# Attention in halves of 64 tokens: eight small score tiles at once, half as many weighted scores, two state steps per block

## The chip, the cores and the metric

The kernel runs on one core of one Trainium2 chip. The metric is the device time of one execution in microseconds (us). A run of the program is longer than its span in the profile, because some time lies before the first and after the last instruction that the profile shows.

## The reference, cut to what matters

The inputs are x (4 batches, 8 heads, 768 tokens, 32 values), a decay a per token, and B and C (16 values per token). The attention is linear with decay; the reference works in chunks of 32 tokens:

```python
cum = np.cumsum(la, axis=-1)                      # la = log(a) of the chunk
L = np.exp(cum[:, :, :, None] - cum[:, :, None, :]) * causal
M = np.einsum('bhin,bhjn->bhij', Cc, Bc) * L      # scores, weighted
y = einsum(M, xc) + einsum(Cc, state) * exp(cum)  # inside the chunk + from the state
state = decay_full * state + sum_j(Bc * xc * decay_from_j)
```

The result is independent of the size of the chunk. Behind it stands a feed-forward layer over the 256 values of a token (8 heads of 32): normalise with the gain g, multiply by w1 (256 x 1024), relu, multiply by w2 (1024 x 256), add the input. The weights come as 64-bit pairs of words and are rebuilt in the kernel.

## The kernel before, in words

The 768 tokens are worked in six blocks t = 0 to 5 of 128 tokens; a block of all four batches is 512 columns. Inside a block the decays are kept per sub-block of 32 tokens (SUB). Nothing is planned at run time: a list of 645 steps, ISSUE, is written out in full, and each engine and the DMA queue of SyncE (SP) execute their own steps strictly in that order. A step that waits holds up everything behind it on its engine. A step's name stands for a function (L496 to L505 hold the table).

Attention of a block, in the names of the steps:

- `C`, `cm`, `B` (L318 to L334) scale C and B by decays inside a sub-block; `cm` parts the heads into even and odd ones. `c2` (L336) is C for the state's part, `be` (L342) is B decayed to the end of the block.
- `W` (L347) copies the decays between sub-blocks into the weights WW, with three copies on ScalarE for each half u of the batches.
- `G t u` (score, L352) is TensorE's: for each of two batches and each pair of heads q, B (32 rows, 128 columns of weights) against C of two heads (256 columns). Four pairs of heads lie in four groups of 32 rows of the array. A block needs `G t 0` and `G t 1`, each with four tiles of PSUM.
- `R t u q` (weighted, L364) is one VectorE multiplication of a PSUM tile (128 x 512) by WW: eight per block.
- `V t n` (value, L369) makes y for batches n and 2+n: for t > 0 first the state's part (L382: 32 rows, 64 columns of weights, 128 columns streamed), then the part inside the block (L387: 128 rows, 32 columns of weights, 128 columns streamed).
- `Z t` (carry, L390) sums B times x over the 128 tokens (128 rows, 32 columns, 64 columns streamed); `K` (L399) and `S` (L403) step the state once per block on VectorE, `sb` (L410) masks the state by head.
- `y`, `yh`, `yl`, `T`, `tc` copy y out of PSUM, split it in two parts, and turn it to tokens; `st`, `ag`, `rs`, `rc` are the statistics of the normalisation.

Every multiplication of fp32 operands on TensorE appears in the trace as two matmul records, each with its own load of weights; those of fp32r operands as one.

The feed-forward layer of a block is `h t m` (hidden, L459; eight per block, six matmuls of 512 columns each), `hh` on ScalarE and `hl` on VectorE, then `o t b` (outputs, L475; four per block, 24 matmuls of 256 columns each), `oe` on VectorE and the store `od`. The weights are prepared ahead of the first block: `k0` to `k3`, `kr`, `f` rebuild a quarter of w1 or w2, `wc`, `wh`, `wl` centre and split it. `fill` (L489) is a matmul of zeros whose result nobody reads. PSUM has five buffers for the attention (`att`) and three for everything else (`ffn`).

## Time and profile before

| what | value |
|---|---|
| three runs: median (lowest, highest) | 208.12 us (207.79, 210.56) |
| the profiled execution's own time | 208.15 us |
| its span, first to last instruction | 206.1 us |
| granted TensorE clock, mean of the span | 0.975 of full |
| TensorE matmul (PE) busy | 194.9 us, 95%, 1,874 records |
| VectorE (DVE) busy | 134.8 us, 65%, 280 instructions |
| ScalarE (ACT) busy | 88.1 us, 43%, 166 instructions |
| GpSimd (POOL) busy | 30.2 us, 15%, 29 instructions |

The ends of matmul records are modelled and records overlap, so a sum of their busy times is more than the time they hold TensorE. The chain of work that ended last gives the time of a group of records from its first start to the start of the next group; those figures add up to the span.

### The profile page before, as it was taken

To read this page: it belongs to the slowest core of one execution; us is meant where nothing else is said; L and a number is where in the kernel's file an instruction comes from. 1 tells how busy PE (TensorE), PEld (TensorE's weight loads), DVE (VectorE), ACT (ScalarE), POOL (GpSimd) and SP (SyncE) were. 2 spreads that over 40 slices of the span, in tenths; PEclk is the share of its full clock that TensorE was granted. 3 is DMA by queue.
4 is the path that set the end of the run, shared out by engine and by line. 5 is a ranking of instruction groups with operands and counts; after the bars stand their busy time and mean duration, and the time that the engine had idled before them with its cause. 6 is when DMAs were issued, how large, how long until landed. Compare 5 with 4: busy or idle time off the path is not lost.

```text
span 206.1 us, 4484 instructions
## 1 busy us (share of the span) xinstructions
PE 194.9 (95%) x1874; PEld 163.5 (79%) x1874; DVE 134.8 (65%) x280; ACT 88.1 (43%) x166; POOL 30.2 (15%) x29
## 2 busy tenths in 40 slices
PE   8359999989999999999999999999999999999993
PEld 8246555759887788889877999779898799988993
DVE  5689999999959998747449813662634651547310
ACT  3799897951553875223425212352033310145100
POOL 0216254432261213000000000004000000000000
PEclk9955999999999999999999999999999999999999
DMA  5899974143646020010003011000000001000011
GB/s 160 257 380 390 386 268 151 54 124 101 226 147 241 32 70 38 0 56 27 25 3 102 3 51 51 3 0 29 25 25 29 0 25 49 5 29 2 3 49 51
DMA packets 12180, 18.90 MB, mean 92 GB/s; under 512 B 2528, under 2 KB 6144, under 8 KB 12160
## 3 DMA queue, kind: packets, MB, share of 16 engines
q1 hardware_dynamic: 12160, 18.62, 26.4%
q8 instruction: 14, 0.23, 0.5%
q14 instruction: 6, 0.05, 0.1%
HBM read 15.31 MB, written 3.31 MB: 90 GB/s over the span
## 4 chain that ended last, share of the span: by engine, by line
PE 80%; DVE 7%; DMA 4%; ACT 4%; SPq 2%; issue 2%; ACTq 0%
PE po L480 34%; PE ph L465 28%; PE G L360 6%; PE yps L387 5%; DMA b<-in_bn_dram 4%; PE yps L382 3%; PE yt L434 2%; PE wc L214 2%; DVE R L366 1%; ACT top L178 1%; DVE cs L320 1%; ACT WW L350 1%; PE Z L396 1%; ACT hh L469 1%; ACT L453 1%
## 5 line engine op out<-in xcount | busy, mean ns | idle before, releaser
L480 PE MATMUL po<-w,hh 128*128 128x256 f32 x384 | 68.9, 282 | 0.0
L480 PEld LDWEIGHTS po<-w,hh 128*128 128x128 f32 x384 | 58.7, 188 | 2.9 <-issue 1.9
L465 PE MATMUL ph<-yh,w 128*128 128x512 f32 x192 | 53.6, 401 | 0.9 <-DVE hl L473 0.8
L480 PE MATMUL po<-w,hl 128*128 128x256 f32 x192 | 53.6, 279 | 0.0
L469 ACT ACTIVATE hh<-ph 128x512 fp32r<-128x512 f32 x48 | 28.6, 597 | 55.0 <-PE ph L465 49.9
L473 DVE SCALAR_TENSOR_TENSOR hl<-ph,hh 128x512 fp32r<-128x512 f32 x48 | 32.8, 687 | 21.2 <-ACT hh L469 20.9
L465 PEld LDWEIGHTS ph<-yh,w 128*128 128x128 f32 x192 | 34.3, 188 | 10.0 <-DVE hl L473 1.5
L480 PEld LDWEIGHTS po<-w,hl 128*128 128x128 f32 x192 | 36.1, 188 | 0.0
L484 DVE SCALAR_TENSOR_TENSOR o<-po,rstd,ytok 128x256 f32<-128x256 f32 x24 | 11.5, 481 | 30.5 <-PE po L480 30.5
L366 DVE TENSOR_TENSOR R<-G,WW 128x512 f32<-128x512 f32 x48 | 30.5, 679 | 0.7 <-PE G L360 0.6
L465 PE MATMUL ph<-yl,w 128*128 128x512 f32 x96 | 30.0, 392 | 0.3 <-DVE yl L427 0.3
L350 ACT COPY WW<-wt 32x512 f32<-32x512 f32 (+2 forms) x36 | 19.8, 613 | 17.5 <-DVE R L366 13.6
L465 PEld LDWEIGHTS ph<-yl,w 128*128 128x128 f32 x96 | 18.0, 188 | 4.6 <-DVE yl L427 0.7
L360 PE MATMUL G<-cm,bs 32*128 32x256 f32 x192 | 16.0, 443 | 1.0 <-DVE bs L334 1.0
L360 PEld LDWEIGHTS G<-cm,bs 32*128 32x128 f32 x192 | 10.3, 207 | 4.2 <-issue 1.6
L202 POOL TENSOR_TENSOR top<-top,raw 128x512 int32<-128x512 int32 x8 | 11.2, 1402 | 15.8 <-DVE top L192 7.8
L427 POOL TENSOR_TENSOR yl<-y,yh 128x512 fp32r<-128x512 f32 x3 | 3.8, 1283 | 61.9 <-DVE yh L424 61.9
L387 PE MATMUL yps<-R,xt 128*32 128x128 f32 x384 | 12.8, 275 | 0.1
L387 PEld LDWEIGHTS yps<-R,xt 128*32 128x32 f32 x384 | 9.8, 109 | 1.9 <-issue 1.9
L418 ACT COPY y<-yps 128x256 f32<-128x256 f32 x13 | 4.4, 369 | 14.0 <-PE yps L387 13.8
L446 DVE BATCH_NORM_STATS2 st<-ytok 128x6 f32<-128x256 f32 x24 | 9.2, 415 | 1.7 <-ACT ytok L439 1.7
L439 ACT COPY ytok<-yt 128x512 f32<-128x512 f32 x12 | 7.0, 581 | 4.2 <-PE yt L434 4.2
(87 smaller groups left out, 173.6 us busy)
## 6 DMA issues: line engine op xcount, KB each, us to landing
raw<-in_w_dram SPq DMA_DIRECT2D x8, 512.0 KB, 7.0
xt<-in_x_dram SPq DMA_DIRECT2D x6, 512.0 KB, 5.3
out_dram<-o SPq DMA_DIRECT2D x24, 128.0 KB, 1.7
ud<-scr SPq DMA_DIRECT2D x10, 256.0 KB
c<-in_cn_dram SPq DMA_DIRECT2D x6, 256.0 KB
b<-in_bn_dram SPq DMA_DIRECT2D x6, 256.0 KB, 5.0
bt<-in_bt_dram SPq DMA_DIRECT2D x5, 256.0 KB
a<-in_a_dram SPq DMA_DIRECT2D x1, 256.0 KB
```

The source lines that it names most:

```text
L202: e.tensor_tensor(out=f, in0=f, in1=words.pop((w, *at))[0], op=ALU.add)
L350: nc.scalar.copy(WW[u][:SUB * i, :, :, i].rearrange("p b h k -> p (b h) k"), src)
L360: nc.tensor.matmul(G[q][:, v], bs[r, tok], cm[r, :, tok], start=True, stop=True)
L366: nc.vector.tensor_tensor(out=R.rearrange("p v i k -> p v (i k)"), in0=tiles.pop(("G", t, u, q)).rearrange("p v i k -> p v (i k)"), in1=WW ...
L387: nc.tensor.matmul(tiles["y", t, u, g][32 * k:32 * k + 32, v], x[:, b * NH + h], tiles["R", t, u, h // 2][:, v, h % 2], start=(t == 0), st ...
L439: nc.scalar.copy(tiles["ytok", t][:, u * NV:(u + 1) * NV], tiles.pop(("yt", t, u)))
L446: nc.vector.bn_stats(out=st, in_=tiles["ytok", t][:, b])
L465: nc.tensor.matmul(ph, W1[m // 4, k][:, s, mc], v[:, k], start=(i == 0), stop=(i == len(cmb) - 1))
L469: nc.scalar.activation(h, tiles["ph", t, m], AF.Relu)
L473: nc.vector.scalar_tensor_tensor(out=l, in0=tiles.pop(("ph", t, m)), scalar=0.0, in1=tiles["hh", t, m].bitcast(F32), op0=ALU.max, op1=ALU. ...
L480: nc.tensor.matmul(po, tiles[v, t, m][:, cols], W2[m // 2,][:, s, (m % 2) * DM:(m % 2 + 1) * DM], start=(n == 0), stop=(n == len(cmb) - 1))
L484: nc.vector.scalar_tensor_tensor(out=o, in0=tiles.pop(("po", t, b)), scalar=tiles["rstd", t][:, b], in1=tiles["ytok", t][:, b], op0=ALU.mu ...
```

## The change

A block of 128 tokens is still the unit of the feed-forward layer, but the attention inside it works on two halves f = 0, 1 of 64 tokens.

- `G t` now serves all four batches: for each batch, half and pair of heads the weights are 64 tokens of B (32 rows, 64 columns) and 128 columns are streamed. The half picks the column half of the array, the pair of heads the row group. Scores across the halves are no longer computed; four PSUM tiles hold the whole block.
- `R t q`: four per block instead of eight, of the same size. WW shrinks to one tile with one weight per half (`W t`: two copies of 32 x 1024 instead of six of 32, 64 or 96 x 512); the sums and exponentials behind it (`e`, `x`) shrink from four to two.
- `V t n` handles batches 2n and 2n+1, batch by batch: the state's part for both halves, 64 columns streamed, then the part inside the halves with 64 rows, 32 columns of weights, 64 columns streamed. The two halves are two row groups and write to different PSUM tiles. In block 0 the second half has a state's part too.
- `Z t` gives one sum for each half (64 rows each); in block 5, where there was none, the first half's is needed.
- `K t f`, `S t f`, `sb t f` step and mask the state twice per block.
- `fill` takes the PSUM pool as an argument.
- ISSUE is written anew as a whole: order, engines of some steps, loads. 45 fills stand where 14 stood, all in the head.

The core of the diff (plain renamings and sizes of tiles are cut):

```diff
-    WW = [cp.tile([P, NV, NH, NSUB, SUB], F32, name=f"WW{i}") for i in range(NU)]
+    WW = cp.tile([P, NB, NH, 2, SUB], F32, name="WW")
...
-    def decays(t, u):
-        for i in range(1, NSUB):
-            src = wt[:SUB * i, t, u * NV * NH:(u + 1) * NV * NH, i - 1].unsqueeze(2).to_broadcast([SUB * i, NV * NH, SUB])
-            nc.scalar.copy(WW[u][:SUB * i, :, :, i].rearrange("p b h k -> p (b h) k"), src)
+    def decays(t):
+        for f in range(NF):
+            rows = slice(f * HALF, f * HALF + SUB)
+            nc.scalar.copy(WW[rows, :, :, 1].rearrange("p b h k -> p (b h) k"), wt[rows, t].unsqueeze(2).to_broadcast([SUB, NR, SUB]))
...
+        G = [ps_att.tile([P, NB, 2, HALF], F32, tag="att", name=f"G{t}{q}") for q in range(NQ)]
+        for b in range(NB):
+            for f in range(NF):
+                tok = slice(b * P + f * HALF, b * P + (f + 1) * HALF)
+                for q in range(NQ):
+                    r = slice(2 * DS * q, 2 * DS * (q + 1))
+                    nc.tensor.matmul(G[q][f * HALF:(f + 1) * HALF, b], bs[r, tok], cm[r, :, tok], start=True, stop=True)
...
+        for b in range(2 * n, 2 * n + 2):
+            for f in range(NF):
+                for q in range(NQ if t + f > 0 else 0):
+                    r, d = slice(2 * DS * q, 2 * DS * (q + 1)), slice(q % 2 * 2 * HD, (q % 2 + 1) * 2 * HD)
+                    tok = slice(b * P + f * HALF, b * P + (f + 1) * HALF)
+                    nc.tensor.matmul(tiles["y", t, q // 2, f][d, b], tiles["sbd", t, f][r, b], c2[r, tok], start=True, stop=False)
+            for g in range(KC):
+                for k in range(4):
+                    for f in range(NF):
+                        h, r = 4 * g + k, slice(f * HALF, (f + 1) * HALF)
+                        nc.tensor.matmul(tiles["y", t, g, f][32 * k:32 * k + 32, b], x[r, b * NH + h], tiles["R", t, h // 2][r, b, h % 2],
+                                         start=(t + f == 0), stop=True)
...
+                for f in range(NF if t < NT - 1 else 1):
+                    h0, r = b * NH + 2 * q, slice(f * HALF, (f + 1) * HALF)
+                    nc.tensor.matmul(tiles["Z", t, f][32 * q:32 * q + 32, b], be[r, h0:h0 + 2].rearrange("p h n -> p (h n)"),
+                                     x[r, h0:h0 + 2].rearrange("p h d -> p (h d)"), start=True, stop=True)
...
+    def before(t, f):
+        return (t, f - 1) if f else (t - 1, NF - 1)
...
-    def fill(i):
+    def fill(i, bank):
```

The head of the new order, up to the first hidden tile:

```diff
+ini:v, ld a, inv:v, az:p, ld mask, fill 0 ffn, ld w1 1 1, fill 1 ffn, fill 2 ffn, ld b 0, fill 3 ffn, fill 4 ffn, ld sums, fill 5 ffn, fill 6 ffn,
+ld g, fill 7 ffn, fill 8 ffn, clip, ld la, fill 9 ffn, ones:a, fill 10 ffn, u, ld w1 0 1, fill 11 ffn, fill 12 ffn, ld c 0, fill 13 ffn, fill 14 ffn,
+ld w1 0 0, fill 15 ffn, iv, fill 16 ffn, ld sel, d, fill 17 ffn, k0 1 1 1, fill 18 ffn, ld id, fill 19 ffn, fill 20 ffn, ld bt 0, kr 1 1 1,
+fill 21 ffn, fill 22 ffn, k1 1 1 1, ld x 0, cf, fill 23 ffn, B:v 0, fill 24 ffn, ld w1 1 0, fill 25 ffn, fill 26 ffn, ld w2 0, k2 1 1 1, fill 27 ffn,
+l1, fill 28 ffn, k3 1 1 1, l2, l3, so, f:p 1 1 1, ld b 1, kr 1 0 1, fill 29 ffn, fill 30 ffn, sm, ld b 5, k0 1 0 1, fill 31 ffn, fill 32 ffn, C:v 0,
+fill 33 ffn, fill 34 ffn, fill 35 ffn, k1 1 0 1, cm:a 0 1, fill 36 ffn, l4, k2 1 0 1, e 0, cm:a 0 0, k3 1 0 1, e 1, x 0, G 0, f:p 1 0 1, ld w2 1,
+kr 1 0 0, ld bt 1, x 1, gm, k0 1 0 0, ld c 2, fill 37 ffn, fill 38 ffn, mb:p, W 0, ld as, k1 1 0 0, sp, be:v 0, fill 39 ffn, k2 1 0 0, fill 40 ffn,
+ld w2 2, fill 41 ffn, k3 1 0 0, fill 42 ffn, fill 43 ffn, em, fill 44 ffn, R 0 3, f:p 1 0 0, R 0 1, Z 0, ld w2 3, kr 1 1 0, R 0 2, wc 0 0, k0 1 1 0,
+c2 0, S 0 0, k1 1 1 0, ld bt 4, k0 2 0, R 0 0, sb:p 0 1, kr 2 0, ld x 2, wc 0 1, k1 2 0, W 1, k2 1 1 0, ld c 1, k2 2 0, k3 1 1 0, k3 2 0, V 0 0,
+K 0 1, wh 1 0 0, S 0 1, f:p 1 1 0, kr 2 1, wl:v 1 0 0, V 0 1, k0 2 1, be:v 1, wh 1 0 1, sb:v 1 0, ld bt 2, wl:v 1 0 1, wc 1 0, f:p 2 0, ld x 1,
+y:a 0 0 0, y:a 0 1 0, y:v 0 1 1, kr 2 2, y:v 0 0 1, yh:v 0 1, yh:a 0 0, K 1 0, wh 2 0, wc 1 1, yl:v 0 1, kr 2 3, k1 2 1, rcl, wh 1 1 0, k2 2 1,
+yl:v 0 0, h 0 0, wh 1 1 1, wl:v 1 1 0, k3 2 1, h 0 1, wl:v 1 1 1, f:p 2 1, hh 0 0, hl 0 0, h 0 7, wl:v 2 0, wh 2 1, ru, hh 0 1, wl:v 2 1, k0 2 2,
+ro 0, h 0 2, hl 0 1, hh 0 7, be:p 2, k0 2 3, hl 0 7, h 0 6, riv, hh 0 2, k1 2 2, ld bt 3, rd, hl 0 2, ro 1, h 0 3, k1 2 3, hh 0 6, k2 2 2, k2 2 3,
...
```

## Rows read from the trace of the kernel before

**Rows 1.** Two stages: busy us by engine, clock, DMA share, GB/s.

```profile
10.00:20.00 10.00, 7.23 (x44) 5.38 (x44) 8.68 (x19) 9.73 (x23) 4.19 (x4) 0.52 1.02 381
...
40.00:50.00 10.00, 9.22 (x67) 7.51 (x67) 9.66 (x17) 4.37 (x8) 4.61 (x4) 1.00 0.34 107
```

**Rows 2.** TensorE's waits: us in total, times, longest.

```profile
PE ph L465 <- DVE hl L473: 0.8, 1, 0.8
```

**Rows 3.** Chain that ended last: start, length (us), work.

```profile
4.96 8.11 DMA b<-in_bn_dram
...
43.28 1.65 PE ph L465 x6
...
44.93 1.08 PE G L360 x16
...
46.01 5.88 PE po L480 x48
...
191.60 11.21 PE po L480 x96
```

**Rows 4.** The same chain, attention: state part, value part, two carries.

```profile
55.96 0.60 PE yps L382 x16
...
56.55 1.01 PE yps L387 x32
...
71.16 0.58 PE Z L396 x32
...
74.96 0.45 PE Z L396 x32
```

**Rows 5.** Records on TensorE by form: busy us, mean ns, idle before.

```profile
L360 PE MATMUL G<-cm,bs 32*128 32x256 f32 x192 | 16.0, 443 | 1.0 <-DVE bs L334 1.0
...
L382 PE MATMUL yps<-c,sbd 32*64 32x128 f32 x160 | 6.7, 280 | 0.0
...
L387 PE MATMUL yps<-R,xt 128*32 128x128 f32 x384 | 12.8, 275 | 0.1
...
L396 PE MATMUL Z<-xt,be 128*32 128x64 f32 x160 | 3.2, 221 | 0.0
```

**Rows 6.** VectorE by form, same columns: what goes.

```profile
L366 DVE TENSOR_TENSOR R<-G,WW 128x512 f32<-128x512 f32 x48 | 30.5, 679 | 0.7 <-PE G L360 0.6
...
L171 DVE COPY WW<-cst 128x2048 f32<-128x2048 f32 x1 | 1.2, 1202 | 0.0
...
L446 DVE BATCH_NORM_STATS2 st<-ytok 128x6 f32<-128x256 f32 x24 | 9.2, 415 | 1.7 <-ACT ytok L439 1.7
```

**Rows 7.** VectorE by form: what comes, or comes in more often.

```profile
L344 DVE TENSOR_TENSOR be<-bt,pend 128x512 f32<-128x512 f32 x4 | 2.6, 680 | 0.0
...
L338 DVE SCALAR_TENSOR_TENSOR c<-cs,em 128x512 f32<-128x512 f32 x5 | 3.4, 682 | 0.0
...
L412 DVE TENSOR_TENSOR sbd<-S,cst 128x256 f32<-128x256 f32 x4 | 1.7, 418 | 0.0
...
L223 DVE TENSOR_TENSOR w<-wc,w 128x512 fp32r<-128x512 f32 x4 | 2.7, 665 | 0.0
...
L418 DVE COPY y<-yps 128x256 f32<-128x256 f32 x11 | 4.2, 416 | 4.9 <-PE yps L387 4.9
...
L424 DVE CAST yh<-y 128x512 fp32r<-128x512 f32 x6 | 2.8, 476 | 0.9 <-ACT y L418 0.9
...
L401 DVE TENSOR_TENSOR K<-S,emt 128x256 f32<-128x256 f32 x4 | 1.6, 410 | 0.0
```

**Rows 8.** GpSimd's mask and ScalarE's copy of decays, by form.

```profile
L412 POOL TENSOR_TENSOR sbd<-S,cst 128x256 f32<-128x256 f32 x1 | 2.2, 2222 | 7.5 <-DVE S L408 7.5
...
L350 ACT COPY WW<-wt 32x512 f32<-32x512 f32 x12 | 7.4, 613 | 17.5 <-DVE R L366 13.6 <-DVE mv L449 3.9
```

**Rows 9.** TensorE in order of time, the first fills: start, length, form, count.

```profile
0.77 5.03 PE L492 MATMUL idle<-const-float32-0.0 128*128 128x128 f32 x22 [0.77 <-PEq L578]
```

**Rows 10.** The page's DMA queues: packets, MB, share: instruction loads.

```profile
q8 instruction: 14, 0.23, 0.5%
```

More of the change, by code (lines that the diff above doesn't have):

```diff
@@ L410, in diagonal @@
-    def diagonal(t, e=nc.gpsimd):
-        sb = tiles["sbd", t] = p2.tile([P, NB, 2 * HD], F32, tag="sbd", name=f"sbd{t}")
-        e.tensor_tensor(out=sb, in0=tiles["S", t], in1=blkt.unsqueeze(1).to_broadcast([P, NB, 2 * HD]), op=ALU.mult)
-    def gathered(t, u, g, e=nc.scalar):
+                for f in range(NF if t < NT - 1 else 1):
+                    h0, r = b * NH + 2 * q, slice(f * HALF, (f + 1) * HALF)
+                    nc.tensor.matmul(tiles["Z", t, f][32 * q:32 * q + 32, b], be[r, h0:h0 + 2].rearrange("p h n -> p (h n)"),
+                                     x[r, h0:h0 + 2].rearrange("p h d -> p (h d)"), start=True, stop=True)
@@ new lines, in before, with kept, state_of @@
+    def before(t, f):
+        return (t, f - 1) if f else (t - 1, NF - 1)
+    def kept(t, f):
+        S = tiles["K", t, f] = p1.tile([P, NB, 2 * HD], F32, tag="K", name=f"K{t}{f}")
+        nc.vector.tensor_tensor(out=S, in0=tiles[("S", *before(t, f))], in1=emt[:, t, f].unsqueeze(2).to_broadcast([P, NB, 2 * HD]), op=ALU.mult)
+    def state_of(t, f):
+        S = tiles["S", t, f] = p2.tile([P, NB, 2 * HD], F32, tag="S", name=f"S{t}{f}")
+        if t + f == 0:
+            nc.scalar.copy(S, tiles["Z", t, f])
+        else:
+            nc.vector.tensor_tensor(out=S, in0=tiles["Z", t, f], in1=tiles["K", t, f], op=ALU.add)
@@ L415, in gathered, with diagonal @@
+    def diagonal(t, f, e=nc.gpsimd):
+        sb = tiles["sbd", t, f] = p2.tile([P, NB, 2 * HD], F32, tag=f"sbd{f}", name=f"sbd{t}{f}")
+        e.tensor_tensor(out=sb, in0=tiles[("S", *before(t, f))], in1=blkt.unsqueeze(1).to_broadcast([P, NB, 2 * HD]), op=ALU.mult)
+    def gathered(t, g, f, e=nc.scalar):
         if ("y32", t) not in tiles:
             tiles["y32", t] = p1.tile([P, KC, TB], F32, tag="y32", name=f"y32{t}")
-        dst = tiles["y32", t][:, g, u * NV * P:(u + 1) * NV * P]
-        (e.copy if e is nc.scalar else e.tensor_copy)(dst, tiles.pop(("y", t, u, g)).rearrange("p v k -> p (v k)"))
+        dst = tiles["y32", t][:, g].rearrange("p (b f k) -> p b f k", b=NB, f=NF)[:, :, f]
+        (e.copy if e is nc.scalar else e.tensor_copy)(dst, tiles.pop(("y", t, g, f)))
@@ L429, in turned @@
     def turned(t, u):
[L430 to L431 removed]
+        ps = tiles["yt", t, u] = ps_att.tile([P, 2, DM], F32, tag="att", name=f"yt{t}{u}")
+        for v in range(2):
             for g in range(KC):
[L433 removed]
+                tok = slice((2 * u + v) * P, (2 * u + v + 1) * P)
                 nc.tensor.transpose(ps[:, v, g * P:(g + 1) * P], tiles["y32", t][:, g, tok], ident)
```

178 lines of the change are left out of this document (69 added, 109 removed).

## The prediction, made before the changed kernel ran

> **What bounds the kernel now.** I read the busy shares first, then the stretches of 10 us, then the chain of waits and TensorE's own waits. The stretches show two regimes. From 10 to 20 us TensorE is busy for 7.2 of 10 us at a granted clock of 0.52, while ScalarE is busy for 9.7 and VectorE for 8.7; from 40 to 50 us TensorE has 9.2 and VectorE still 9.7 [rows 1]. The last time TensorE waits for another engine is 0.8 us for `hl` of block 0 [rows 2], just before the chain goes over to TensorE at 43.28 us. From 44.93 us the chain is TensorE without a break, up to the last output group that begins at 191.60 and lasts 11.21: to 202.81 us, with one VectorE operation and a store behind it [rows 3]. So what the change does after about 45 us is worth exactly the TensorE time that it takes away; what it does before that is worth what VectorE, the fuller of the other engines, is spared. The sum is made against the profiled execution's 208.15 us (span 206.1), which stands 0.03 above the median of the runs, 208.12.
>
> **A price for small matmuls.** The value part and the carry load weights of the same shape (128 rows, 32 columns) and have 32 records each; one streams 128 columns and takes 1.01 us, the other 64 and takes 0.58 [rows 4]. 32 records with 64 columns fewer save 0.43 us: 0.21 ns per column and record, and 0.15 us remain for changing the shape of the tile (32 x 64 x 0.21 = 0.43; 0.58 - 0.43). The other two forms fit the same slope. 16 records of the state's part with 128 columns are 0.43, of 0.60 [rows 4]: 0.17 fixed. 16 score records with 256 columns are 0.86, of 1.08 [rows 3]: 0.22 fixed. Each of these four forms has four tiles of the array to fill (four row groups, or four column groups, or a diagonal of 32 x 64), and a record's own length is 219 to 443 ns [rows 5] while they start 14 to 68 ns apart. I read the slope as four tiles working side by side, 0.84 ns per column in each. The change makes tiles of 32 x 64 (scores) and 64 x 32 (values, carry), of which eight fit. **The choice:** I take eight side by side, 0.105 ns per column and record, because row groups alone and column groups alone each gave the full factor of four in these rows, and the loops go through eight different tiles in turn. The state's part keeps four tiles. The trace shows no case of eight, so four remains the other bound.
>
> **TensorE in blocks 1 to 5.** Per block, new:
> - Scores: 64 records x 128 columns x 0.105 = 0.86, + 0.17 = 1.03 us, for two groups of 1.08.
> - State's part, now batch by batch: 16 records x 64 x 0.21 = 0.215, + 0.17 = 0.385, four times = 1.54, for two of 0.60. It becomes dearer: four groups pay the fixed part, not two.
> - Value part: 32 records x 64 x 0.105 = 0.215, + 0.15 = 0.365, four times = 1.46, for two of 1.01.
> - Carry: 64 records x 64 x 0.105 = 0.43, + 0.15 = 0.58, as before. In block 5 a new one comes, 32 records in one row group: 0.58.
>
> Before, from 44.93 us on: 10 x 1.08 + 10 x 0.60 + 10 x 1.01 + three carries (0.58 + 0.45 + 0.45 [rows 4]) = 28.4 us. After: 5 x (1.03 + 1.54 + 1.46) + 5 x 0.58 = 23.05. I charge all five carries, though two of them now stand ahead of the first output. **Difference: -5.35 us.** Hidden, output, turning and store groups are untouched.
>
> **The head, by VectorE up to the last `hl` of block 0.** By the two orders, gone are four `R` (4 x 0.68), the copy of masks (1.20) and two `st` (2 x 0.415): 4.75 us [rows 6]. Ahead of the same point now come one `be` 0.68, `c2` 0.68, one `sb` 0.42, one `wl` 0.67, one `y` 0.42, one `yh` 0.48: 3.35 [rows 7]. **Difference: -1.4 us** for the first output group; two `ag` and an `rc` go as well, which I leave out. This holds if VectorE's idle time in the first 13 us stays. Its new ends: the two loads that the first scores need, b 0 and c 0, are fourth and ninth in SP's queue. The chain before shows b 0 landing at 13.07 us after 8.11 us, as the tenth issue [rows 3], with 2.55 MB ahead of and including it by the sizes of the tiles; c 0 now has 2.05 MB. So the data are not later, and could be 20% of 8.1, or 1.6 us, earlier. I take nothing for it, because `C` of block 0 moves from GpSimd to VectorE, where everything behind it (a quarter of w1, `be`, `R`) now waits for that load.
>
> **Edits costed at nothing, and their cover.** 31 more fills (62 records): 22 records took 5.03 us at the start [rows 9], 0.23 each, so 62 would be 14 us; at the full clock half. TensorE has that room while it waits for loads, and the clock of 0.52 in 10 to 20 us [rows 1] is what they fill. If the clock is not granted, they reach past 20 us and delay `wc`: up to 3.5 us. `V 0 0` newly waits for the masked state of the first half: `Z 0`, a copy, and `sb` on GpSimd, 2.22 us [rows 8]. Behind it in TensorE's queue are all later `wc` and `h`. `wc 0 0` and `wc 0 1` run ahead of it as cover; without them 2.2 us are lost. Block 0's values also get a state's part (+0.5 us net), hidden as VectorE is the later one there. `W` is two copies of twice the length, at most 2 x 1.23 us a block against 6 x 0.61 [rows 8]; ScalarE has room after 40 us. Per block VectorE loses four `R` (2.7) and gains a `K` and an `S` of the same size (0.82) [rows 6, 7]; it does not become the bound. SP's order moves the loads of `ud` behind `bt 3` and the stores of decays; they are needed first by block 1's scores, which come behind two output groups of 2.9 us each. Instruction loads on q8 grow from 14 by the ratio of records: 1,874 become about 2,892 (scores 192 to 384, values 384 to 768, state 160 to 352, carry 160 to 352, fills +62, sums -4), so some 8 more. The 14 took 0.5% of 16 engines, 1.2 us each [rows 10], and no wait of TensorE after 45 us stands against them [rows 2]: between nothing and 9.4 us, and I take nothing.
>
> **Sum:** 208.15 - 5.35 - 1.4 = 201.4 us, -3.2%.
>
> **Rivals.**
> - *Only four tiles at a time.* The row and column splits do not combine. Then scores cost 64 x 128 x 0.21 + 0.17 = 1.89, values 4 x (0.43 + 0.15) = 2.32, carries 1.01: blocks 1 to 5 take 5 x (1.89 + 1.54 + 2.32) + 4 x 1.01 + 0.58 = 33.4 us, 5.0 more than before, and block 0 gives back the head's gain: 213.2 us, slower. Between 23.05 and 33.4 the body breaks even at about 5.3 tiles at once (10.3 of the 23.05 us scale with their number), and below that it loses. For it: no row shows eight, and two halves write the same PSUM partitions. Against: the four row groups of the scores do so now, at the same slope. Chance 0.08.
> - *A floor on the spacing.* Records cannot start closer than the closest that the trace shows, the carry's 0.45 us for 32 or 14 ns [rows 4]. Scores at 13.4 ns keep their gain; values become 2.32 and carries 1.01 as above: 5 x (1.03 + 1.54 + 2.32) + 4.62 = 29.1, +0.7 us, and the head's -1.4 is used up by block 0: about 208.5, no change. Chance 0.11. The Trainium skill names such a floor (TensorE: Matmul & The Clock Gate, section "Wait — 56ns, not 53.3ns?"): start to start never below about 25 ns, however few the columns. By that figure, as an estimate, blocks 1 to 5 would need 47 us and the run 227. The carry's 14 ns speak against it.
> - *The gain is given back by new waits in the head.* Fills at the low clock (3.5) and the exposed `sb` (2.2) make 207.1 at most, 204 to 207. For it: the order is new throughout and VectorE was nearly full. Chance 0.15.
> - What I have not thought of, instruction loads among it: 0.05, on either side.
>
> **How the numbers follow.** The forecast has 0.61: 201.4. Its own range is 198.5 (loads 1.6 us earlier, some fixed parts overlapped) to 204. The range 198.5 to 209 takes in the second and third rivals and leaves out the first. Two per cent, about what a measurement can tell from no change, is 204.0 and 212.3. Faster: the forecast and a little of the third rival, 0.64. Same: the second and most of the third, 0.26. Slower: the first and half of the unknown, 0.10.
>
> **What would show it.** In the changed chain: scores as groups of 64 records in 1.0 us (1.9 if four tiles), values 32 records in 0.37 (0.58), carries 64 in 0.58 (1.0), state's part 16 in 0.39. The first output group should start near 44.5 us, `V 0 0` without a wait for GpSimd, and the granted clock in 10 to 20 us near 1. I am wrong if those groups are long, if TensorE shows waits after 45 us, or if the first output group starts after 46 us.

## The result, and the profile after

The changed kernel takes 206.21 us (median of 20 runs, 204.56 to 209.33); the kernel before, run beside it, 208.34 (20 runs, 207.32 to 210.56). The ratio is 0.989, 95% interval 0.986 to 0.992: 1.1% faster, where 3.2% were forecast. Four of the 20 executions are over 1.5% above the fastest; the ratios leave such executions out, the medians do not. The profiled run is the median one, 206.2 us with a span of 204.2: 1.95 us below the profiled run of before, where the sum said 6.75.

The same two stages as [rows 1]: busy us by engine, granted clock, DMA share, GB/s.

```profile
10.00:20.00 10.00, 8.84 (x179) 7.13 (x177) 9.30 (x18) 8.52 (x18) 4.61 (x5) 1.00 1.02 364
40.00:50.00 10.00, 10.00 (x188) 9.04 (x187) 9.25 (x22) 5.53 (x10) 4.45 (x4) 1.00 0.43 138
```

From 10 to 20 us, behind the fills, the clock was granted at its upper level (1.00, that is 2.4 GHz, where 0.52 stood). VectorE is about as full as before (8.68 and 9.66 us in the two stages before).

The chain that ended last (start, length, work), the rows that answer to [rows 3, 4]:

```profile
24.67 1.37 issue
...
27.05 5.33 PE wc L218 x8
...
61.43 1.43 DVE yh L436
...
72.67 2.22 DVE yl L439 x2
...
74.93 0.50 PE ph L478
...
82.70 1.14 PE G L365 x63
...
116.12 0.39 PE yps L387 x16
116.51 0.38 PE yps L392 x32
...
126.04 0.54 PE Z L403 x32
...
127.31 0.41 issue
```

The reader is to see three things. The small matmuls came out at the forecast's size: 64 scores in 1.14 us (1.03 said), 32 values in 0.38 (0.365), 16 of the state's part in 0.39 (0.385), 32 carries in 0.54. The chain is not TensorE without a break from 45 us: until 75 us it leaves TensorE again and again, mostly for VectorE. And twice TensorE stands for "issue", that is for nothing that the profile names, in the middle of a run of small matmuls.

The small groups also show the eight tiles directly. In the kernel before, four records of the value part (128 columns) start 7 ns apart, and the next four begin 109 ns after the first of them (the first round of a group takes a little longer). In the changed kernel it is eight scores of 128 columns that start 7 ns apart, and the next eight begin 109 ns after the first of them; in its values (64 columns) eight follow eight after 56 ns. From about the 36th record of a group of scores these rounds end, and the starts are some 16 ns apart (13.6 in the rounds): that is part of why scores cost more than the sum says.

TensorE in order of time, from the first output matmul to block 3's scores, first in the kernel before:

```profile
45.94 0.50 PE L480 MATMUL po<-w,hh 128*128 128x256 f32 x2
...
82.83 1.15 PE L360 MATMUL G<-cm,bs 32*128 32x256 f32 x16
```

Then in the changed kernel, and its waits over the whole run:

```profile
45.61 0.51 PE L493 MATMUL po<-w,hh 128*128 128x256 f32 x2
...
72.07 0.85 PE L447 MATMUL yt<-cst,y 128*128 128x128 f32 x4
72.67 1.31 PE L478 MATMUL ph<-yh,w 128*128 128x512 f32 x4
74.33 1.10 PE L478 MATMUL ph<-yl,w 128*128 128x512 f32 x2 [0.35 <-DVE yl L439]
75.27 0.60 PE L447 MATMUL yt<-cst,y 128*128 128x128 f32 x4
...
82.63 1.21 PE L365 MATMUL G<-cm,bs 32*64 32x128 f32 x64
```

```profile
PE yps L392 <- issue: 1.8, 2, 1.4
...
PE ph L478 <- DVE yl L439: 0.4, 1, 0.4
PE G L365 <- DVE S L419: 0.2, 1, 0.2
```

The list of waits gives VectorE 0.6 us. The order of time shows more: six hidden matmuls begin at 72.67 and the next group at 75.27, 2.60 us for what takes 1.4 to 1.5 elsewhere. A wait inside a group of overlapping records is hidden in their modelled ends; the distance between starts shows it.

Those six wait for the two `yl` of block 2, and GpSimd (POOL) has a part in that:

```profile
61.11 1.47 POOL L439 TENSOR_TENSOR yl<-y,yh 128x512 fp32r<-128x512 f32 x1
61.40 1.47 DVE L436 CAST yh<-y 128x512 fp32r<-128x512 f32 x1
...
72.27 1.46 POOL L338 TENSOR_TENSOR bs<-b,ud 128x512 f32<-128x512 f32 x1 [5.51 <-DMA ud<-scr]
72.62 2.26 DVE L439 TENSOR_TENSOR yl<-y,yh 128x512 fp32r<-128x512 f32 x2
```

The first of the two `yl` took 1.66 us, where one takes 0.68 elsewhere, while GpSimd worked on `B` of block 5; the `yh` above it took 1.47 instead of 0.42. From 46 to 83 us five VectorE instructions of the changed kernel are clearly longer than the shortest of their kind, by 3.2 us together, each while a GpSimd instruction runs; in the kernel before it is one, by 0.3. VectorE counts as busy for as long as they last.

**Where the gain went.** Block 3's scores are a point that both kernels reach with the same work done, but for one turning (four short matmuls) that the changed kernel has done already. The kernel before reaches it at 82.83 us, the changed one at 82.63. Against the forecast:

| stretch | before | forecast | after |
|---|---|---|---|
| to the first output matmul | 45.94 | -1.4 | 45.61: -0.33 |
| from there to block 3's scores | 36.90 | -2.65 | 37.02: +0.12 |
| from there to TensorE's end | 119.96 | -2.76 | 118.19: -1.77 |

(The forecast's 5.35 us are divided by the groups that lie in each stretch; 0.08 go to the carries that now stand ahead.) Missing are 1.1, 2.8 and 1.0 us. In the middle stretch, where nothing was won, VectorE is nearly full in both kernels; the row of the kernel before stands first, the changed one's second:

```profile
46.00:83.00 37.00, 37.00 (x471) 30.81 (x474) 33.37 (x72) 18.31 (x35) 10.79 (x8) 1.00 0.37 121
```

```profile
46.00:83.00 37.00, 36.27 (x702) 30.02 (x708) 33.74 (x75) 17.72 (x31) 9.93 (x9) 1.00 0.45 141
```

VectorE was busy for 33.4 of 37 us and still is (33.7), although half the `R` went: the new order gave it `K` and `S` twice per block, more statistics, and `B`, `yh` and `cm` steps that ScalarE or GpSimd had done, and 3.2 us of the 33.7 are the lengthening just told.

For the gaps, the page's row that answers to [rows 10]:

```profile
q8 instruction: 22, 0.36, 0.8%
```

22 loads of 16 KB for the 2,892 matmul and 2,892 weight-load instructions of TensorE: about 260 to a load, so an instruction is some 64 bytes and a load some 256 of them. The eight-tile groups use that up fast: half a block's values are 192 instructions in 1.5 us. In the trace the load whose instructions end the 1.37 us gap landed at 24.75 us; TensorE went on at 26.04.

Counting TensorE's instructions through a trace (matmuls, weight loads and the few semaphore ones) settles what these gaps are. In the changed kernel and the 16 further traces of it and its versions below, 60 records of scores, values, carries or outputs start more than 0.25 us after the record before them on the same line. Fifty-two of them have a number that is 192 or 193 above a multiple of 256, in block 0's values number 705 and in block 4's 4,289, and in all 52 TensorE goes on 1.2 to 1.7 us after a 16 KB load has landed. The other eight are block 1's scores, which wait for `S`.

### The profile page after: what moved, and what is told of

Read it like the earlier page. It is cut to its first block, busy times and chain, and to the rows that moved or that the text cites. A ratio compares the mean times of both kernels' runs of the same rounds, so it can differ in the third digit from the quotient of the medians.

```text
span 204.2 us, 6505 instructions
## 1 busy us (share of the span) xinstructions
PE 195.4 (96%) x2892; PEld 167.5 (82%) x2892; DVE 132.4 (65%) x273; ACT 80.2 (39%) x138; POOL 30.9 (15%) x33
## 4 chain that ended last, share of the span: by engine, by line
PE 72%; DVE 10%; DMA 7%; ACT 4%; SPq 2%; issue 2%; DVEq 0%
PE po L493 30%; PE ph L478 25%; PE wc L218 4%; PE yps L392 4%; PE yps L387 4%; DMA ud<-scr 3%; DMA c<-in_cn_dram 3%; PE G L365 2%; ACT WW L354 2%; PE yt L447 1%; DVE yl L439 1%; PE Z L403 1%; DVE hl L486 1%; DVE yh L436 1%; DVE cs L324 1%
## 5 line engine op out<-in xcount | busy, mean ns | idle before, releaser
L478 PEld LDWEIGHTS ph<-yh,w 128*128 128x128 f32 x192 | 35.1, 188 | 7.6 <-issue 0.4
L354 ACT COPY WW<-wt 32x1024 f32<-32x1024 f32 x12 | 12.5, 1043 | 11.8 <-DVE R L371 10.6
L371 DVE TENSOR_TENSOR R<-G,WW 128x512 f32<-128x512 f32 x24 | 15.1, 680 | 0.7 <-PE G L365 0.7
L506 PE MATMUL idle<-const-float32-0.0 128*128 128x128 f32 x90 | 12.9, 302 | 1.4 <-PEq L593 0.8
L506 PEld LDWEIGHTS idle<-const-float32-0.0 128*128 128x128 f32 x90 | 11.9, 212 | 2.0 <-issue 0.9
L392 PE MATMUL yps<-R,xt 64*32 64x64 f32 x768 | 11.4, 222 | 1.8 <-issue 1.8
L424 POOL TENSOR_TENSOR sbd<-S,cst 128x256 f32<-128x256 f32 x7 | 5.3, 763 | 44.8 <-DVE S L419 43.9
L387 PE MATMUL yps<-c,sbd 32*64 32x64 f32 x352 | 10.6, 230 | 0.0
L392 PEld LDWEIGHTS yps<-R,xt 64*32 64x32 f32 x768 | 7.2, 106 | 3.7 <-issue 2.1
```

Source lines behind the costliest of these rows:

```text
L354: nc.scalar.copy(WW[rows, :, :, 1].rearrange("p b h k -> p (b h) k"), wt[rows, t].unsqueeze(2).to_broadcast([SUB, NR, SUB]))
L371: nc.vector.tensor_tensor(out=R.rearrange("p b i k -> p b (i k)"), in0=tiles.pop(("G", t, q)).rearrange("p b i k -> p b (i k)"), in1=WW.re ...
L387: nc.tensor.matmul(tiles["y", t, q // 2, f][d, b], tiles["sbd", t, f][r, b], c2[r, tok], start=True, stop=False)
L392: nc.tensor.matmul(tiles["y", t, g, f][32 * k:32 * k + 32, b], x[r, b * NH + h], tiles["R", t, h // 2][r, b, h % 2], start=(t + f == 0), s ...
L478: nc.tensor.matmul(ph, W1[m // 4, k][:, s, mc], v[:, k], start=(i == 0), stop=(i == len(cmb) - 1))
L506: nc.tensor.matmul(ps.tile([P, P], F32, tag=bank, name=f"idle{i}"), zero.to_broadcast([P, P]), zero.to_broadcast([P, P]), start=True, stop ...
```

## The experiments

Each expectation uses letters for its theories, which hold for the runs of its own group; I name them in words: the *load theory* (instructions come late where small matmuls stand close), the *VectorE theory* (VectorE is the bound up to block 3's scores), the *cover theory* (the new order leaves TensorE too little other work where it waits).

### Eight tiles or four

`four_tiles`: the halves f go to the outermost loop in scores, values and carry, so that neighbours share a half.

```diff
-        for b in range(NB):
-            for f in range(NF):
+        for f in range(NF):
+            for b in range(NB):
```

> The changed kernel with the loop over the halves outermost in scores, values (inside a batch) and carry: the same matmuls, but neighbours in the order use four different tiles of the array, not eight. Theory A (eight tiles work side by side, and that is the gain): scores 64 records in 1.9 us instead of 1.14, values 32 in 0.58 instead of 0.38, carry 64 in 1.0 instead of 0.54; over blocks 1 to 5 about 9 us more, 213 to 216 us. Theory B (the records' spacing is set by issue, whatever the tile): no group changes by more than 0.1 us and the time stays at 206.

208.49 us, ratio 1.000 (0.996 to 1.004). Its chain:

```profile
93.39 1.55 PE G L365 x64
...
107.47 1.66 PE Z L403 x111
...
118.12 0.41 PE yps L392 x29
```

Scores take 1.55 instead of 1.14, values 0.41 instead of 0.38, two carries 1.66 instead of 1.41. The order of the loops is worth the whole gain, though neither of the sizes expected came. About half of the rounds of the scores are now four records in 109 ns; in the middle of a group a second round of four starts 5 or 6 ns behind the first, so part of the work still goes eight at a time. The values hardly change (0.41 where four tiles would give 0.58): what speaks for eight tiles there is the rounds of eight in 56 ns, not this run.

### Where the gap in block 0's values comes from

`fills28` and `fills14`: the first 28 or 14 fills cut into two of 64 columns, more instructions for the same columns.

```diff
-        nc.tensor.matmul(ps.tile([P, P], ...), zero.to_broadcast([P, P]), zero.to_broadcast([P, P]), ...)
+        for w in range(parts):  # 2 for the first 28 (14) fills, else 1
+            nc.tensor.matmul(dst[:, cols], zero.to_broadcast([P, P]), zero.to_broadcast([P, P // parts]), ...)
```

> The changed kernel, but each of the first 28 fills is two matmuls of 64 zero columns instead of one of 128: the same TensorE work, 112 more instructions ahead of block 0's values. Theory A (TensorE ran out of loaded instructions in the middle of block 0's values: 1.4 us at 24.7 us, and the clock fell behind it, 1.7 us on the weight centring): a block of 256 instructions now ends near the start of the values and the next one in the hidden tiles, so the gap of 1.4 us is gone or under 0.3 us, the eight centring records after the values take 3.7 us, not 5.3, and the first output group starts at 43 to 44 us, not 45.6; about 2 us less in all. Theory B (VectorE sets the first output group): the gap may go, but the first output group still starts after 45.2 us and the time is within 0.5 us of the changed kernel's.

> The changed kernel, only the first 14 fills cut in two: 56 more instructions ahead of block 0's values. Theory A: the gap does not go, it moves to 56 instructions earlier in the values, so at about 23.8 us, and is longer by what those take, 1.4 + 0.5 = about 2 us. Theory C (the gap is a wait for data, for the masked state or x): it stays before the same matmul, batch 2's second half of the values, with 1.4 us.

223.73 us (ratio 1.072, 1.064 to 1.080) and 219.56. Not the test it was meant to be: the fills held TensorE until 25.4 us.

```profile
0.77 24.66 PE L509 MATMUL idle<-const-float32-0.0 128*128 128x64 f32 x114 [0.77 <-PEq L596]
```

114 records in 24.66 us are 0.216 each, as long as fills of 128 columns in [rows 9]: half the columns took no less time. In the changed kernel the fills of 128 columns go from 0.21 us each to 0.11 at about 4 us, where the clock's upper level begins (3.77 us); here that level begins at 29.14 us, in `fills14` at 16.40. So the edit also kept TensorE at the lower level (before its first record the clock column reads 1.00; the spacing of the fills is the evidence). With the head that much later the data loads were over and the gap in block 0's values was gone, but another of 2.6 us stood in block 2's values.

`tiny28`: fills 14 to 27 as three matmuls of 32 x 8 each, 112 more instructions in no more time.

```diff
+        if 14 <= i < 28:
+            for w in range(3):
+                nc.tensor.matmul(dst[:32, 8 * w:8 * w + 8], zero.to_broadcast([P, 32]), zero.to_broadcast([P, 8]), ...)
```

> The changed kernel; fills 14 to 27 are each three matmuls of 32 weight columns and 8 streamed columns instead of one of 128 and 128: 112 more instructions ahead of block 0's values, and no more TensorE time (84 records at about 31 ns for 28 at about 107). Theory A (TensorE's gap in block 0's values is a late load of instructions): the gap of 1.4 us in the values goes or falls under 0.4 us and the eight centring records behind them take 3.1 to 3.7 us, not 5.3. Theory A1 (gap and clock set the first output group): it starts at 42.5 to 43.5 us, not 45.6, and the time falls by 2 to 3 us. Theory A2 (VectorE sets it, the gap is hidden in its wait): TensorE waits for VectorE in block 0's hidden tiles instead, the first output group starts at 44.5 to 45.6 us, and the time falls by less than 1 us.

209.14 us, ratio 0.998 (0.993 to 1.003). The gap in block 0's values shrank to 0.2 us, and three others opened where the changed kernel had none, in block 1's values, in an output group, and in block 2's values (0.79 at 75.34); the one in block 4's values is gone. The first two:

```profile
57.60 0.53 issue
...
60.79 2.99 issue
```

Instructions that do nothing, some 50 us earlier and more, moved the gaps, and their numbers are again 192 or 193 above a multiple of 256: they go with the count of instructions, not with data, buffers or semaphores. The time says little: the small fills left the clock at 0.68 from 10 to 20 us (1.00 in the changed kernel), and the profiled execution took 210.27 us.

`after_again`: the changed kernel once more, nothing edited.

> The changed kernel as it is, once more. Theory C (late instruction loads): the same instructions leave gaps of another size, since a load's landing depends on what the data queues carry at that moment; block 0's values again have the gap ahead of the same record (1.37 us in the first profile), now anywhere between 0.4 and 1.5, and the groups without a gap keep their times within 0.05 us (scores 1.14, state part 0.39, values 0.38). Rival (the gap is a wait of the order, on a product or a buffer): 1.37 again within 0.1.

205.97 us. The same instructions leave other gaps, none of them in block 0's values:

```profile
PE po L493 <- issue: 0.9, 1, 0.9
...
PE G L365 <- issue: 0.7, 1, 0.7
PE yps L392 <- issue: 0.6, 1, 0.6
```

The last one is again in block 4's values. So whether a load lands in time depends on the execution, more than expected: in block 0's values the expectation had a gap of at least 0.4 us. The first output came at 44.49 us here, where 44.5 was forecast; block 0's scores, which wait for the first data loads, also began 0.46 us earlier than in the first profile (12.87 for 13.33).

### VectorE up to block 3's scores

`late_turn`: `h 1 4` and `h 1 2` ahead of block 2's turning, as cover; their `hh` and `hl` stay where they were.

```diff
-B:p 5, st 1 3, h 1 7, ag 1 2,
+B:p 5, st 1 3, h 1 7, h 1 4, h 1 2, ag 1 2,
```

> The changed kernel with two hidden tiles of block 1 (h 1 4, h 1 2) moved in TensorE's order ahead of the turning of block 2's y; nothing else moves on VectorE. Theory A (between 70 and 75 us TensorE waits in its order for VectorE's y of block 2, with work at hand that stands behind): the 1.7 us that the turning and the first hidden tile of block 2 take too long are gone; 1 to 1.7 us less. Theory B (VectorE is the bound there and all of TensorE's work hangs on it): the wait comes back at the next hidden tiles, and the time is within 0.5 us of the changed kernel's.

207.06 us, ratio 0.990 (0.986 to 0.995); block 3's scores at 82.72. The wait came back elsewhere:

```profile
PE ph L478 <- DVE hl L486: 1.9, 3, 1.0
```

I took that for the VectorE theory. `cover`, below, moves the `hh` and `hl` as well, and there the waits at this place are gone.

`relief`: six steps from VectorE to ScalarE, four `cm` and two `yh` (later expectations speak of four).

```diff
-cm:v 2 1, ... yh:v 1 0, ... cm:v 3 1, yh:v 1 1, ... cm:v 4 0, cm:v 4 1,
+cm:a 2 1, ... yh:a 1 0, ... yh:a 1 1, cm:a 3 1, ... cm:a 4 0, cm:a 4 1,
```

> The changed kernel with six steps of blocks 1 to 4 moved from VectorE to ScalarE at the same places of the order: the rounding of block 1's y (two), and four of the parted C (blocks 2, 3, 4). VectorE's profiled time for them is 4.1 us, all between 55 and 72 us. Theory A (from 46 to 83 us VectorE is the bound of the changed kernel, so TensorE's gain in blocks 1 and 2 is lost): block 3's scores start 1.5 to 3 us earlier than 82.6 us, and the time falls by as much. Theory B (TensorE's own work, loads of instructions and the order are the bound there): block 3's scores start within 0.5 us of 82.6 us and the time stays within 0.6 us of the changed kernel's.

205.79 us, ratio 0.987 (0.983 to 0.991).

```profile
46.00:83.00 37.00, 36.25 (x740) 30.33 (x739) 30.36 (x67) 20.79 (x37) 8.05 (x7) 1.00 0.46 137
```

VectorE 3.4 us less, block 3's scores at 81.35 us, 1.3 earlier. But 1.0 of the 1.3 lies ahead of the first output matmul (44.62 for 45.61), where none of the moved steps stands; from there to block 3's scores it took 36.73 us for 37.02, and the waits at block 2's turning stayed. So this is not the VectorE theory's 1.5 to 3 us. The lowest median but one, but its interval overlaps the changed kernel's.

`nostats_before` and `nostats_after`: the statistics of block 1 (`st`, `ag`) left out in either kernel.

> The kernel before, with the same four st and ag steps of block 1 left out. Both theories: TensorE was the bound there before the change, so block 3's first scores start within 0.4 us of 82.9 us and the time does not change. If they start over 1 us earlier, VectorE was the bound already before, and the trace of before, which shows no wait of TensorE after 43 us, was read wrongly.

> The changed kernel without the statistics of block 1 (its four st and ag steps are left out, a constant stands for the variance): 2.3 us less work for VectorE between 66 and 72 us, nothing else. Theory A (VectorE is the bound there): TensorE's waits at the turning and first hidden tile of block 2 shrink and block 3's scores start 1 to 2 us earlier. Theory B: within 0.4 us of 82.6 us.

Before: 208.82 us, ratio 1.001 (0.998 to 1.004), block 3's scores at 83.02 against 82.83: as expected, VectorE was no bound there. After: 207.77, 0.994 (0.991 to 0.998), block 3's scores at 84.37, later and not earlier. Its chain and waits show what stood in the way:

```profile
46.45 1.93 issue
```

```profile
PE yt L447 <- ACT y L430: 1.6, 1, 1.6
```

A miss: the gaps of the loads are larger than what was to be measured.

### Both together

`carries_apart` (`relief`, with block 2's carry behind block 0's first output group), `relief2` (`relief`, with five more steps from VectorE to GpSimd), and `relief2_apart` (both):

```diff
-tc 0 0, Z 2, wl:p 2 2, S 1 0, o 0 0,
+tc 0 0, wl:p 2 2, S 1 0, o 0 0, Z 2,
```

```diff
-be:v 1, ... sb:v 1 0, ... be:v 4, ... C:v 4, ... C:v 5,
+be:p 1, ... sb:p 1 0, ... be:p 4, ... C:p 4, ... C:p 5,
```

> The version with four steps moved from VectorE to ScalarE, and block 2's carry behind block 0's first output group instead of right behind block 1's carry. Theory C: the instructions of the first output group then have 3 us more to arrive in (24 output matmuls of 0.125 us lie between the carries); the gap ahead of output matmul 7, 0.48 us in the version it is made from, 0 to 2.2 in others, is gone, and no other comes in its place; the whole comes to 203.9 to 205.8, mean 205.2. Rival (the gap is paid by a wait for hh or hl): it stays at 0.5 or more, 205.8. Theory A (VectorE bounds to block 3) by itself: state steps S 2 0 and S 2 1 come 3 us later and VectorE idles before them, block 3's scores no earlier than 81.4.

> The version with four steps moved from VectorE to ScalarE, and five more moved from VectorE to GpSimd (block 1's beta and its first widened state, block 4's beta, the key-side scans' products C of blocks 4 and 5: 0.78 + 0.42 + 0.78 + 2 x 0.78, together 3.5 us of VectorE's time, 1.2 of it ahead of 46 us). GpSimd has 1.8 us busy of 64 to 83. Theory A: first output group 0.4 to 1.2 us earlier than 44.6, block 3's scores 1 to 2.5 us earlier than 81.35; whole 203.5 to 205. Rival (VectorE is no longer the bound there, the waits of the first four steps were all of it): block 3's scores within 0.5 us of 81.35, whole 205.8. Below that: GpSimd's own time for a 128x512 product, 2 us and more, is late for one of them, or slows VectorE by its accesses: slower by up to 2 us.

> Both: nine steps off VectorE, and block 2's carry behind block 0's first output group. If A and C both hold and add: 202.5 to 204.5; if only A: as the version with nine steps moved; if only C: 0.5 us below the version with four.

206.58 us (ratio 0.990, 0.986 to 0.993), 206.27 (0.991, 0.986 to 0.996), 207.39 (0.994, 0.990 to 0.998): none as low as expected. The chain of the last:

```profile
47.57 3.00 PE po L493 x24
...
61.30 0.82 PE G L365 x36
62.12 1.18 issue
```

The gap behind the carries is gone (24 output matmuls in 3.00), as the load theory says, and a larger one stands in the next group of scores. Nor did five steps more off VectorE bring block 3's scores forward: 82.40 in `relief2`, 83.56 in `relief2_apart`. (The trace of `carries_apart`, used in the table below, is of an execution of 208.01 us.)

`cover`: `relief`, with `h 1 7` between the halves of block 2's values, `h 1 4` and `h 1 2` behind them, and their `hh` and `hl` moved forward as well.

```diff
-V 2 0, ... V 2 1, ... h 1 7, ... T 2 1, hh 1 7, yl:v 2 1, h 2 0, tc 2 1, hl 1 7,
+V 2 0, h 1 7, ... V 2 1, ... hh 1 7, ... hl 1 7, ... h 1 4, ... h 1 2, ... T 2 1, yl:v 2 1, hh 1 4, h 2 0, tc 2 1, hl 1 4,
```

> The version with four steps moved from VectorE to ScalarE (205.8; block 3's scores at 81.35), and hidden tiles of block 1 put around block 2's values: h 1 7 between the two halves of the values, h 1 4 and h 1 2 (2.8 us) behind them, ahead of block 2's turning and h 2 0, with their hh and hl in the same order. Theory A (in 69 to 75 us TensorE waits for VectorE's and ScalarE's work on block 2's y, because the new order leaves it too little other work there): the waits between 69 and 75 us, 1.8 us in that version (6 hidden 2.14, turning 1.10, 6 hidden 1.83 against 1.45, 0.36 and 1.45), fall under 0.5; block 3's scores at 79.6 to 80.4; whole 204.0 to 205.0. Theory B (VectorE is full there, and what is put ahead only moves its waits): block 3's scores at 81.0 or later, the wait for hl or yl elsewhere, whole 205.8.

205.70 us, ratio 0.987 (0.982 to 0.993). TensorE in order of time:

```profile
72.48 1.19 PE L478 MATMUL ph<-yh,w 128*128 128x512 f32 x4
...
75.34 0.60 PE L447 MATMUL yt<-cst,y 128*128 128x128 f32 x4
75.69 1.17 PE L478 MATMUL ph<-yh,w 128*128 128x512 f32 x4
...
77.16 0.60 PE L447 MATMUL yt<-cst,y 128*128 128x128 f32 x4
```

The waits of 69 to 75 us are gone: 12 hidden matmuls in 2.86, the turning in 0.35, 6 in 1.47. So far the cover theory is right. Yet from the first output to block 3's scores it took 36.68 us, as long as `relief`: this execution lost 0.8 us in block 0's values and 1.0 behind the carries to late instructions, and 0.7 to VectorE's `hl` just ahead of block 3's scores, which stood at 82.41.

`spread` (`cover`, the carries apart, and half an output group between the halves of block 1's values) and `spread_alone` (the same without the six steps of `relief`):

```diff
-V 1 0, c2 2, ... V 1 1, ... o 0 1,
+V 1 0, c2 2, ... o 0 1 0, V 1 1, ... o 0 1 1,
```

> The same with the short matmuls apart as well: block 2's carry behind block 0's first output group, and half of block 0's last output group (12 matmuls, 1.5 us) between the halves of block 1's values, so that no more than 200 short records stand in a row between 42 and 75 us. Theory C (gaps come where a run of short records uses up its 256 instructions before the next 256 have landed): no gap over 0.2 us between 42 and 75 us in the groups of values and outputs, where the versions before had 0.3 to 3.3; scores at 1.14 each; with A, block 3's scores at 79 to 80 and the whole 203.0 to 204.5. Rival (the loads are late whatever the order, because the data loads hold the queues): gaps of 0.5 to 2 us in all, in other places; whole as the version without, or above.

> Both changes of order (hidden tiles around block 2's values, short matmuls apart), but the four steps back on VectorE as in the changed kernel. Theory A: VectorE has 2.4 us more between 46 and 80 us; block 3's scores 0.7 to 1.5 us later than with the steps moved, whole 204 to 205.5. Theory C alone (the loads were all): the same as with the steps moved, within 0.3.

206.55 us (0.992, 0.989 to 0.996) and 206.39 (0.990, 0.987 to 0.993). From 42 to 75 us values, carries and output groups run without a gap, but the two groups of scores take 1.98 and 2.12 us in the one, 1.87 and 2.17 in the other, instead of 1.14; issue has 0.6 and 0.7 us of it, waits for `S` 0.4 and 0.3. With or without the relief makes no difference here (38.39 and 38.27 us from the first output to block 3's scores): a second time six steps fewer on VectorE win nothing in that stretch.

### Where neither data loads nor VectorE disturb

`tail_alone` moves only steps behind 115 us; `tail_cover` is the same in `cover`.

```diff
-rc 3, Z 5, V 4 1, S 5 0, sb:p 5 1, h 3 6,
+rc 3, h 3 6, Z 5, V 4 1, S 5 0, sb:p 5 1, h 3 0,
...
-rc 4, V 5 1, o 3 1,
+rc 4, o 3 1, V 5 1,
```

> The changed kernel with two moves behind 115 us, where TensorE alone bounds and the data loads are over: h 3 6 (6 hidden matmuls, 1.4 us) between the first half of block 4's values and block 5's carry, h 3 0 behind the second half, and one output group (24 matmuls, 2.9 us) between the halves of block 5's values. The work is the same. Theory C: the gap inside block 4's values, at the same place in each version so far (32 records in 0.98 to 1.09 us instead of 0.38), is gone, because 6 long matmuls stand ahead of the second half; the wait for issue behind 83 us falls from 0.4 to 0.6 us to nothing, and from block 3's scores to the end it takes 117.3 to 117.7 us instead of 118.2. Rival (the gap belongs to the change between values and carry, or to a wait for the state): it stays, 118.2.

> The same two moves, with the four steps moved to ScalarE and the hidden tiles around block 2's values (205.7 without the two moves, 36.7 us from the first output group to block 3's scores, 118.2 from there). Theories A and C: 117.3 to 117.7 for the last stretch, 36.0 to 37.0 for the one before, the whole 204.6 to 205.4. Rival (what is saved behind 83 us is lost to a gap elsewhere): 205.7 or more.

206.03 us (0.988, 0.984 to 0.991) and 206.62 (0.990, 0.986 to 0.994). The chain of the first:

```profile
125.19 1.59 PE ph L478 x6
126.78 0.58 PE Z L403 x32
127.36 0.39 PE yps L387 x16
127.75 0.38 PE yps L392 x32
...
130.41 1.77 DVE yl L439
132.18 0.61 DVE hl L486
```

The gap in block 4's values, which stood at the same place in every kernel that has this order here, is gone in both, and no issue is left behind 83 us: the cleanest showing of the load theory, in a stretch where the queues are nearly empty (DMA share 0.08 behind 83 us). But the last stretch took 118.6 us instead of 118.2: `hl` of `h 3 6` stands behind a `yl` on VectorE that took 1.77 us (the last two rows; 0.68 elsewhere, 1.77 in the changed kernel too, both times with a `yl` on GpSimd beside it), and TensorE waits 0.5 us for the buffer that it frees. In `tail_cover` block 0's values lost 1.3 us to one gap again.

### The versions side by side

Starts of the first output matmul and of block 3's scores, and the rest up to TensorE's end. Late: by how much the groups of values, scores, carries and outputs between block 0's values and block 3's scores took longer than the shortest of their kind in any version, block 0's values included. It is issue, except for block 1's scores and the output matmuls ahead of them, which wait for `S` and `cm`: that is 0.6 to 0.9 us of it in `changed`, `carries_apart`, `spread`, `spread_alone` and `tail_alone`, and 1.6 in `relief2`. Where the carries are apart, one of them (0.7 us) has moved into the middle stretch.

| version | median us | first output | to block 3's scores | rest | late |
|---|---|---|---|---|---|
| before | 208.34 | 45.94 | 36.90 | 119.96 | no issue |
| changed | 206.21 | 45.61 | 37.02 | 118.19 | 2.3 |
| changed, again | 205.97 | 44.49 | 38.03 | 118.08 | 2.3 |
| late_turn | 207.06 | 44.99 | 37.73 | 118.30 | 1.7 |
| relief | 205.79 | 44.62 | 36.73 | 118.52 | 1.0 |
| relief2 | 206.27 | 44.90 | 37.49 | 118.68 | 1.9 |
| carries_apart | 206.58 | 44.40 | 39.34 | 118.92 | 1.8 |
| relief2_apart | 207.39 | 43.71 | 39.85 | 118.49 | 2.6 |
| cover | 205.70 | 45.73 | 36.68 | 118.16 | 1.9 |
| spread | 206.55 | 44.19 | 38.39 | 118.25 | 2.5 |
| spread_alone | 206.39 | 43.96 | 38.27 | 118.18 | 2.4 |
| tail_alone | 206.03 | 44.63 | 37.15 | 118.63 | 1.3 |
| tail_cover | 206.62 | 45.40 | 37.63 | 118.67 | 4.2 |

No version is beyond doubt faster than the changed kernel.

## Why the prediction was right about the tiles and wrong about the whole

- **Eight tiles side by side: right.** Every price was within 0.13 us of the sum's, the starts go in rounds of eight, and `four_tiles` takes the gain back. The first two rivals fell: scores and values are not at their four-tile prices, and 64 carries in 0.70 us (two blocks' in 1.41) are 11 ns apart, 32 in 0.54 with the change of tile. The Trainium skill's floor of about 25 ns from start to start (TensorE: Matmul & The Clock Gate, section "Wait — 56ns, not 53.3ns?") does not hold for these tiles: 32 values in 0.38 us are 12 ns.
- **The failed step is "from 44.93 us the chain is TensorE without a break ... So what the change does after about 45 us is worth exactly the TensorE time that it takes away".** It was read from the chain of the kernel before and carried over to a kernel with another order and less TensorE work. The prediction's own sign of being wrong, waits of TensorE after 45 us, came. Of the 2.8 us missing in the middle stretch, in the profiled execution and by groups: 0.9 in hidden tiles and 0.4 in turnings that wait for VectorE's `yh` and `yl`, 0.6 in scores that wait for `S` (VectorE) and `cm` (ScalarE), 0.4 for one turning that now lies in this stretch, and some 0.4 in sizes (scores 1.14 for 1.03, values 3.08 a block for 3.00). None of it is a late instruction there. That TensorE waits for VectorE's products is shown; that VectorE's full load (33.7 of 37 us) is the reason is not: `relief` takes 3.4 us from VectorE and shortens the stretch by 0.3 (36.73 for 37.02), and `cover`, which also removes the waits at 69 to 75 us, shortens it no further (36.68).
- **"It does not become the bound" (VectorE) failed for the same reason.** I netted `R` against `K` and `S`, and did not count the steps that the new order moves to VectorE, nor the 3.2 us by which VectorE's instructions are longer beside GpSimd's. That lengthening alone accounts for 1.0 of the 1.1 us lost at block 2's turning (one `yl` of 1.66 us for 0.68). No run takes GpSimd's steps away to test it.
- **Instruction loads, "between nothing and 9.4 us, and I take nothing": the other missing term.** In the changed kernel's profile they are 1.4 us in block 0's values and 0.7 in block 4's; in the versions they are what the table's last column holds beside the waits named there. The 22 loads (14 + 8) were forecast to the piece; that they would be late was not, since in the kernel before none was. Shown by the numbers of the instructions at which all of them stand, `tiny28` (they move with the count), `after_again` (they differ between executions of one program), `carries_apart` and `tail_alone` (long matmuls between the short ones remove them there).
- **The head: right within its spread.** 44.5 was forecast; 45.61 came in the first profile and 44.49 in the second of the same kernel, and versions with the same head lie between 44.49 and 45.73, so a hit to 0.01 us is luck. The first profile has the gap of 1.37 us and the fallen clock behind it, but they need not be all of the 1.1: `cover` reaches its first output at 45.73 with a gap of about 0.8 and the clock at 1.00. No wait of `V 0 0` for the masked state appears, and the clock in 10 to 20 us was 1.00. The third rival (fills past 20 us, `sb` exposed) did not come, though 206.21 lies in its 204 to 207: new waits came, but most of them behind 45 us.
- **The rest:** 1.0 us missing behind 83 us is 0.7 around the gap in block 4's values, 0.3 in scores, 0.3 in carries (two blocks' in 1.41 where the sum has 1.16) and 0.2 in values, less 0.5 in turnings, one of which moved out of this stretch.

What stays open: why taking work from VectorE, or waits from TensorE, did not shorten the middle stretch, and how much GpSimd's instructions beside VectorE's cost there. The gaps vary from execution to execution by as much as the effects of the edits, there is one trace of each version, and no edit removed all gaps at once.

## What to carry to other kernels

A chain that is one engine without a break says what bounds the work as it is ordered, and not what bounds it when that engine gets faster: before crediting a saving in full, add up the next fullest engine over the same stretch (33.4 of 37 us here) and ask which of its products the faster engine will wait for. When steps move between VectorE and GpSimd, look for instructions that became longer, not only for the busy share. Splitting matmuls into more tiles that run side by side pays in TensorE time, and costs instructions; where some 200 of them pass in 1.5 us, look for "issue" in the chain. Long matmuls between the groups removed the gap at their place each time here, though the whole became no faster. When cover is moved ahead of a wait, move the steps that free its buffers as well.

## What the hardware showed that I had not expected

- Late instruction loads: TensorE went on 1.2 to 1.7 us after a 16 KB load had landed; the longest gap of all was 2.99 us. They are late where the data loads fill the queues (DMA share 1.07 from 20 to 24 us), but no less often at 127 us, where they don't: all 12 traces with this order there have that gap.
- Behind the gap in block 0's values the granted clock fell. The stages of the changed kernel:

```profile
20.00:24.00 4.00, 4.00 (x87) 1.95 (x85) 4.00 (x8) 3.36 (x5) 1.43 (x2) 1.00 1.07 392
24.00:28.00 4.00, 2.63 (x100) 1.56 (x83) 3.90 (x8) 2.72 (x7) 2.04 (x2) 0.96 0.51 188
28.00:32.00 4.00, 4.00 (x8) 1.73 (x6) 4.00 (x10) 2.53 (x5) 0.00 (x0) 0.62 0.62 195
```

  TensorE was busy for 2.63 of 4 us, then ran for a while at the lower level (1.2 GHz; 0.62 is the mean of both). The eight `wc` took 5.33 us in the chain, against 3.63 in `nostats_after`, whose gap was 1.23 us and whose clock stayed at 1.00 there; in `tail_cover`, behind 1.33 us, it fell. Of the 16 executions under 208 us, the 11 whose mean clock was 0.995 or more have a median of 205.75 us, the 5 others 206.21.
- Fills of 64 columns took as long as those of 128 at the lower clock, 0.216 us each, when each loads 128 columns of weights; 112 more instructions of them and the clock's upper level began at 29.14 us, not at 3.77.
- A VectorE instruction that runs beside one of GpSimd's can take over twice its time (`yl` 1.66 to 1.78 us for 0.68); the multiplications `R`, which read PSUM, kept their 0.68 us beside GpSimd's `C` at 53.8 to 55.6 us.
